# Loading the last two V of a two-block decode attention into the K tiles instead of the V ring

## The chip, the cores and the metric

One core of one Trainium2 chip. The metric is the device time of one launch in microseconds (us). The kernel before takes 1975.22 us (median of 3 runs: 1973.39 to 1975.72).

## The reference

Two independent decode attentions, A and B, with the same shapes; the results are concatenated. One query per batch row, so K and V, 805 MB of bf16 in all, are read once and used once.

```python
# per block: B=2, Sq=1, D=640, H=32 heads, Sk=8192, Dh=192
q = (x @ wq).reshape(B, 1, H, Dh)
scores = einsum("bhqd,bhkd->bhqk", q, k_cache) * Dh ** -0.5
p = softmax(scores)
o = einsum("bhqk,bhkd->bhqd", p, v_cache).reshape(B, 1, H * Dh) @ wo
```

## The kernel before

A *unit* is one head of one batch row of one block: 2 x 32 x 2 = 128 units, 0 to 127. "K126" is the K of unit 126, 3.1 MB laid out as 128 partitions x 64 keys x 192. Per unit, VectorE and ScalarE form the scores from K (VectorE multiplies, products `d1a` and `d1b`, then sums), the softmax follows, and TensorE (PE) makes 32 matmuls of the weights with V. All K and V go through SyncE's DMA queue, into two K tiles and two V tiles used in turn.

```python
kb = [sb(f"kb{i}", [128, T, Dh], BF16) for i in range(NK)]   # NK = 2
vb = [sb(f"vb{i}", [128, T, Dh], BF16) for i in range(NV)]   # NV = 2
# ... cut ...
def pe_pv(u, j0, j1):                      # 32 matmuls of a unit, or a part of them
    b = u % B
    vv = vb[u % NV][:].rearrange("p (j a) d -> p j (a d)", a=2)
    def fn(eng):
        for j in range(j0, j1):
            ins = eng.matmul(ops[(u // B) % 2][0:33, b, 0:QW], pb[u % NPB][:, j, :], vv[:, j, :],
                             start=(j == 0), stop=(j == T // 2 - 1))
        return ins
# ... cut: a V tile may be filled again when the matmuls that read it are done ...
def add_v(u):
    pc = pieces(u)
    w = [key("pv", u - NV)]
    if pc is None:
        S_sp.add(sp_v(u), waits=w)
    else:
        for (t0, t1, sm) in pc:            # the last four units: in 2, 2, 4 and 5 parts,
            S_sp.add(sp_v(u, t0, t1, sm), waits=w)    # each with a semaphore of its own
# ... cut: order on SyncE: K of unit u, then V of unit u-3; at the end
#     K127, V124, V125, V126, V127. K of unit u waits for d1b of unit u-2.
```

Of the kernel before, what the change touches and what calls it, by code (L numbers as in the profile page):

```python
# [102 lines left out]
def build_kernel(nc, blocks, out, cfg=None):  # L103
# [10 lines left out]
    NU = G * B  # L114
# [6 lines left out]
    NK = cfg.get("NK", 2)  # L121
    NV = cfg.get("NV", 2)
# [8 lines left out]
    def unit(u):  # L131
        g = u // B
        return g // Hn, g % Hn, u % B, g
# [14 lines left out]
    with ExitStack() as es:  # L148
# [4 lines left out]
        kb = [sb(f"kb{i}", [128, T, Dh], BF16) for i in range(NK)]  # L153
        vb = [sb(f"vb{i}", [128, T, Dh], BF16) for i in range(NV)]
# [34 lines left out]
        vsem = [sem(f"vsem{i}") for i in range(NV)]  # L189
# [9 lines left out]
        def key(name, *idx):  # L199
            for i in idx:  # L200
                if i < 0:
                    return None
            return (name,) + tuple(idx)
# [13 lines left out]
        def pieces(u):  # L217
            if u not in PCS:
                return None
            n0, cuts = PCS[u]  # L220
            ends = [c * T // 64 for c in cuts]
            return [(t0, t1, vtail[n0 + i]) for i, (t0, t1) in enumerate(zip([0] + ends[:-1], ends))]
# [15 lines left out]
        def dma(out_ap, in_ap, s):  # L238
            return lambda eng: eng.dma_start(out_ap, in_ap).then_inc(s, 16)  # L239
# [25 lines left out]
        def sp_k(u, part=None):  # L265
# [6 lines left out]
                return dma(kb[u % NK][:, 0:ks, :], src[:, 0:ks, :], ksem[u % NK])  # L272
            return dma(kb[u % NK][:, ks:T, :], src[:, ks:T, :], KSPLIT[u])

        def sp_v(u, t0=0, t1=None, sm=None):
            blk, h, b, g = unit(u)
            src = blocks[blk]["v"][b, h].rearrange("(p t) d -> p t d", p=128)
            if t1 is None:
                return dma(vb[u % NV][:], src, vsem[u % NV])
            return dma(vb[u % NV][:, t0:t1, :], src[:, t0:t1, :], sm)  # L280

        def xbc_copy(blk, b):
            return lambda eng: eng.tensor_copy(xbc[blk][b][:], xT[blk][b][:].unsqueeze(2).broadcast_to([128, DC, 128]))
# [87 lines left out]
        def pe_p0(qg):  # L371
            pr, b = qg // 2, qg % 2
            g0 = 2 * pr
            blk = g0 // Hn
            w = g0 // HG
            npr = HG // 2

            def at(slot, off):
                def fn(eng):
                    for c in range(DC):  # L380
                        ins = eng.matmul(qps[:, 0:QW], xbc[blk][b][:, c, :],  # L381
                                         wqs[:, slot, c, off].rearrange("p a n -> p (a n)") if slot is not w % 2 else
                                         wqs[:, slot, c, off],
                                         start=(c == 0), stop=(c == DC - 1))
                    return ins
                return fn
            fn = at(w % 2, slice((pr % npr) * QW, (pr % npr + 1) * QW))
            fn.same = (blk, b)
            fn.turn = lambda it: at(bass.ds((it + pr) // npr % 2, 1), bass.ds((it + pr) % npr * QW, QW))
            return fn, [("wq", w) if w == 0 else None, ("wq0b",) if (w == 0 and WQSPLIT and pr % npr >= 1) else None,  # L390
                        ("xbc", blk), key("a0", qg - 1)]

        def pe_pv(u, j0, j1):
            b = u % B
            vv = vb[u % NV][:].rearrange("p (j a) d -> p j (a d)", a=2)

            def fn(eng):
                for j in range(j0, j1):
# [3 lines that stand above are left out]
            fn.same = (j0, j1)  # L402
            return fn
# [52 lines left out]
        for u in range(NU):  # L456
            g = u // B
            put(dve_tab, u + 1, 0, dve_d3(u), [("acc", u), ("r", u), key("ar", u - 2)], ("d3", u))
            put(dve_tab, u, 2, dve_d1a(u), [("k", u), ("a0", qg_of(u)), key("acc", u - 2)], ("d1a", u))
            put(dve_tab, u, 3, dve_d1b(u), [("k", u), ("kb", u) if u in KSPLIT else None, ("a0", qg_of(u)),  # L460
                                            key("r", u - 1)], ("d1b", u))
            put(dve_tab, u, 4, dve_lvl(u, 96), [("d1b", u)], ("l1", u))
            put(dve_tab, u, 5, dve_lvl(u, 48), [("l1", u)], ("l2", u))
            put(dve_tab, u, 6, dve_lvl(u, 24), [("l2", u)], ("l3", u))
            put(dve_tab, u, 7, dve_r(u), [("l3", u), key("d3", u - 2), key("exp", u - 2)], ("r", u))
            put(pool_tab, u + 1, 0, pool_ar(u), [("d3", u), key("nb", u - 2)], ("ar", u))
            put(pool_tab, u + 1, 1, pool_ls(u), [("exp", u), key("f2", g - 2)], ("ls", u))
            put(act_tab, u + 1, 0, act_nb(u), [("ar", u), key("exp", u - 2)], ("nb", u))
            put(act_tab, u + 1, 1, act_exp(u), [("nb", u), ("acc", u), ("r", u), key("pv", u - NPB)], ("exp", u))
            for t in range(na_of(u)):  # L470
                w = [("d1a", u), key("d3", u - 2), key("exp", u - 2)] if t == 0 else []
                put(act_tab, u, 10 + t, act_acc(u, t), w, ("acc", u) if t == na_of(u) - 1 else None)
            pc = pieces(u)
            w0 = [("exp", u), key("f1", g - 2), ("init",)]
            if pc is None:
                put(pe_tab, u + LATE, 0, pe_pv(u, 0, T // 2), w0 + [("v", u)], ("pv", u))
            else:
                for i, (t0, t1, sm) in enumerate(pc):
                    put(pe_tab, u + LATE, 0, pe_pv(u, t0 // 2, t1 // 2), (w0 if i == 0 else []) + [("vp", u, i)],
                        ("pv", u) if i == len(pc) - 1 else None)  # L480
# [15 lines left out]
        for pp in range(G // 2):  # L496
# [13 lines left out]
            w = [("f4", pp), key("f5", pp - 1)]  # L510
# [8 lines left out]
        for qg in range(NQG):  # L519
            fn, w = pe_p0(qg)  # L520
# [4 lines left out]

        def add_v(u):
            pc = pieces(u)
            w = [key("pv", u - NV)]
            if pc is None:
                S_sp.add(sp_v(u), waits=w)  # L530
            else:
                for (t0, t1, sm) in pc:
                    S_sp.add(sp_v(u, t0, t1, sm), waits=w)
# [15 lines left out]
        for kind, u in korder:  # L549
            if kind == "k":  # L550
                if u in KSPLIT:
                    S_sp.add(sp_k(u, 0), waits=[key("d1b", u - NK)])
                    S_sp.add(sp_k(u, 1))
                else:
                    S_sp.add(sp_k(u), waits=[key("d1b", u - NK)])
                if u == 0:
                    if WQSPLIT:
                        S_sp.add(sp_wq(0, 1))
                    for blk in range(1, NBLK):
                        for b in range(B):  # L560
                            S_sp.add(sp_x(blk, b))
                w = u // UG
                if u % UG == (5 if UG >= 8 else 1):
                    S_sp.add(sp_wo(w), waits=[key("f5", (w - 1) * HG // 2)])
                if u % UG == (3 if UG >= 8 else 0) and w + 1 < NWG:
                    S_sp.add(sp_wq(w + 1), waits=[key("pq", w * HG)])
            else:
                add_v(u)
# [43 lines left out]
def bass_concat_heads__gqa_block_cached__mha_block_cached__decode_kernel(  # L612
    nc: bass.Bass,
    A_x: bass.AP,
    A_k_cache: bass.AP,
    A_v_cache: bass.AP,
    A_wq: bass.AP,
    A_wo: bass.AP,
    B_x: bass.AP,
    B_k_cache: bass.AP,  # L620
    B_v_cache: bass.AP,
    B_wq: bass.AP,
    B_wo: bass.AP,
    out: bass.AP,
):
    blocks = [
        dict(x=A_x, k=A_k_cache, v=A_v_cache, wq=A_wq, wo=A_wo),
        dict(x=B_x, k=B_k_cache, v=B_v_cache, wq=B_wq, wo=B_wo),
    ]
    build_kernel(nc, blocks, out)  # L630
# [28 lines left out]
```

## Time and profile before

| what | number | from |
|---|---|---|
| median time | 1975.22 us | timed runs |
| bytes over the span | 837 MB at 424 GB/s | page |
| V125 issued, its last part landed | 1933.34; 1948.38 us | timeline, chain |
| V126 and V127 issued | 1943.88; 1951.23 us | instruction records of SyncE |
| PE from the landing of V125 to the end of unit 127 | 1948.43 to 1966.58 us | chain |
| end | 1973.2 us | page |

Three lines of the page of the kernel before: the span, the rate in 40 slices of 49 us, and the shares of the chain that ended last (the profile goes back from the last instruction, at each step to what released it).

```profile
span 1973.2 us, 18371 instructions
...
GB/s 384 425 428 427 431 426 429 431 427 430 426 430 430 426 430 427 431 431 424 431 428 429 429 426 432 427 428 426 432 430 426 428 427 432 430 426 429 431 430 292
...
DMA 72%; PE 22%; DVE 5%; issue 1%; SPq 0%; ACT 0%; DVEq 0%
```

Transfers run at about 430 GB/s from the second slice to the last but one. Next, the last 25 us of the chain (start us, length us, what):

```profile
1933.71 14.67 DMA vb<-in_B_v_cache_dram
...
1948.43 2.78 PE ops L399 x16
1951.20 2.18 PE oTps L408 x12
1953.38 6.99 PE ops L399 x32
1960.37 0.91 PE outps L435 x6
1961.27 5.31 PE ops L399 x32
1966.58 1.36 PE oTps L419 x18
...
1970.87 0.43 ACT out_sb L363
```

The DMA piece is V125's second half. From 1948.43 on, no DMA: second half of unit 125, the transposes of an earlier pair of heads (L408), unit 126, that pair's output product (L435), unit 127, then the rest. Finally, busy time by stretches of 4 us (stretch, length, PE, weight load, VectorE, ScalarE, GpSimd, granted PE clock, DMA share, GB/s), and what SyncE's queue did (start, stretch covered by its issues) and waited for from 1930 us on:

```profile
1938.00:1942.00 4.00, 4.00 (x18) 2.01 (x17) 3.97 (x2) 2.45 (x15) 0.00 (x0) 0.69 1.00 423
1942.00:1946.00 4.00, 3.01 (x20) 1.63 (x18) 3.86 (x6) 0.00 (x0) 0.00 (x0) 1.00 0.57 181
1946.00:1950.00 4.00, 3.17 (x20) 1.74 (x19) 0.29 (x2) 0.64 (x3) 0.73 (x2) 1.00 0.99 394
...
1954.00:1958.00 4.00, 4.00 (x16) 1.99 (x15) 0.00 (x0) 0.67 (x2) 0.00 (x0) 0.57 0.98 375
1958.00:1962.00 4.00, 4.00 (x26) 2.13 (x25) 0.00 (x0) 0.64 (x2) 0.00 (x0) 1.00 0.90 359
```

```profile
1943.88 9.73 SPq L239 DMA_DIRECT2D vb<-in_B_v_cache_dram  x9
```

```profile
SPq L239 <- PE ops L399: 28.3, 3, 13.3
```

There is a hole: DMA is 0.57 busy and moves 181 GB/s (bytes counted where packets start; spread over the packets it is 193) in 1942 to 1946, because V126 may not go out before unit 124's matmuls have left its tile. That is what the change goes for.

### The profile page before, as it was taken

What the parts mean: (1) busy time and instruction counts of PE and PEld (TensorE: products, weight loads), DVE (VectorE), ACT (ScalarE), POOL (GpSimd) and SP (SyncE); (2) the same over time, 40 slices, a digit from 0 to 9 for tenths busy, and PEclk for the clock granted to TensorE, in tenths of its full rate; (3) what the DMA queues carried; (4) which work ended last, traced back from release to release, by engine and by line L of the source; (5) the groups of instructions that cost most, each with busy time, mean ns of one, the idle gap of its engine ahead of it and who ended that gap; (6) DMA issues with size and microseconds to landing.
All of it is one profiled execution on the core that took longest, in us unless ns stands there. A gap on an engine that the chain in (4) does not pass through costs nothing.

```text
span 1973.2 us, 18371 instructions
## 1 busy us (share of the span) xinstructions
PE 1116.4 (57%) x5004; PEld 591.5 (30%) x5004; DVE 1655.5 (84%) x962; ACT 904.1 (46%) x4743; POOL 152.7 (8%) x270
## 2 busy tenths in 40 slices
PE   2546546655655555655655656556555565555657
PEld 1223223322333323322332323223232332223324
DVE  7889898888878888888888888888788887888884
ACT  4445454445445444454444444444445444544442
POOL 4013030000000000000000000000000000000000
PEclk9777777777777777777777777777777776777778
DMA  9999999999999999999999999999999999999997
GB/s 384 425 428 427 431 426 429 431 427 430 426 430 430 426 430 427 431 431 424 431 428 429 429 426 432 427 428 426 432 430 426 428 427 432 430 426 429 431 430 292
DMA packets 56477, 837.12 MB, mean 424 GB/s; under 512 B 7417, under 2 KB 18305, under 8 KB 23681
## 3 DMA queue, kind: packets, MB, share of 16 engines
q1 hardware_dynamic: 56432, 836.79, 99.7%
q8 instruction: 12, 0.20, 0.0%
q14 instruction: 17, 0.13, 0.0%
q10 hardware_dynamic: 16, 0.01, 0.0%
HBM read 836.77 MB, written 0.01 MB: 424 GB/s over the span
## 4 chain that ended last, share of the span: by engine, by line
DMA 72%; PE 22%; DVE 5%; issue 1%; SPq 0%; ACT 0%; DVEq 0%
DMA vb<-in_B_v_cache_dram 36%; DMA vb<-in_A_v_cache_dram 29%; PE ops L399 22%; DMA kb<-in_A_k_cache_dram 7%; DVE prodD L303 3%; DVE prodD L310 1%; DVE prodA L299 0%; DVE sc L314 0%; PE oTps L408 0%; PE oTps L419 0%; PE outps L435 0%; SPq L239 0%; SPq L246 0%; DVE mp L306 0%; ACT oTzL L353 0%
## 5 line engine op out<-in xcount | busy, mean ns | idle before, releaser
L399 PE MATMUL ops<-vb,pb 128*33 128x384 bf16 x4096 | 953.2, 408 | 786.7 <-DMA vb<-in_B_v_cache_dram 395.8
L399 PEld LDWEIGHTS ops<-vb,pb 128*33 128x33 bf16 x4096 | 481.4, 120 | 1248.8 <-DMA vb<-in_B_v_cache_dram 414.0
L321 ACT ACTIVATE prodA<-prodA 128x192 bf16<-128x192 bf16 x2048 | 709.1, 350 | 119.0 <-DVE prodA L299 118.6
L303 DVE TENSOR_TENSOR prodD<-kb,qbc 128x9216 bf16<-128x9216 bf16 x128 | 633.7, 4951 | 3.5 <-DMA kb<-in_A_k_cache_dram 3.5
L310 DVE TENSOR_TENSOR prodD<-prodD 128x4608 bf16<-128x4608 bf16 (+2 forms) x384 | 598.9, 1560 | 13.3
L299 DVE TENSOR_TENSOR prodA<-kb,qbc 128x3072 bf16<-128x3072 bf16 x128 | 224.9, 1757 | 250.5 <-DMA kb<-in_B_k_cache_dram 133.4
L321 ACT ACTIVATION_READ_ACCUMULATOR prodA<-prodA 128x1 f32 x2048 | 386.8, 189 | 0.0
L325 ACT ACTIVATE nb<-mg 128x1 f32<-128x1 f32 x128 | 26.0, 203 | 742.2 <-POOL mg L286 742.2
L286 POOL PARTITION_ALL_REDUCE mg<-mp x128 | 57.7, 451 | 1668.7 <-DVE mp L306 1668.7
L314 DVE TENSOR_REDUCE sc<-prodD 128x48 f32<-128x1152 bf16 x128 | 173.1, 1353 | 4.4
L290 POOL PARTITION_ALL_REDUCE lall<-rs x128 | 84.2, 658 | 114.7 <-ACT pb L328 114.7
L335 ACT ACTIVATE o_sb<-ops 1x384 f32<-1x384 f32 x63 | 30.1, 477 | 87.4 <-PE oTps L408 73.3
L408 PEld LDWEIGHTS oTps<-ones,o_sb 33*128 33x128 f32 x372 | 67.1, 257 | 9.8 <-issue 9.8
L408 PE MATMUL oTps<-ones,o_sb 33*128 33x1 f32 x372 | 69.7, 311 | 0.0
L359 ACT ACTIVATE qbc<-qps 128x384 bf16<-128x384 f32 x64 | 31.3, 489 | 79.0 <-PE qps L381 78.3
L328 ACT ACTIVATE pb<-sc,nb 128x64 bf16<-128x64 f32 x128 | 52.2, 408 | 16.6 <-ACT nb L325 8.3
L381 PE MATMUL qps<-wqs,xbc_1 128*128 (+1 forms) x160 | 34.8, 352 | 40.7 <-ACT qbc L359 40.7
L381 PE MATMUL qps<-wqs,xbc_0 128*128 (+1 forms) x160 | 33.2, 340 | 11.8 <-DMA wqs<-in_A_wq_dram 11.8
L306 DVE TENSOR_REDUCE mp<-sc 128x1 f32<-128x64 f32 x128 | 28.1, 220 | 13.9 <-issue 5.0
L435 PE MATMUL outps<-wos,oTz 128*4 (+1 forms) x186 | 31.1, 304 | 14.0 <-ACT oTz L353 14.0
L381 PEld LDWEIGHTS qps<-wqs,xbc_1 128*128 128x128 bf16 x160 | 13.8, 102 | 58.9 <-ACT qbc L359 42.9
L336 ACT ACTIVATE o_sb<-ops 1x384 f32<-1x384 f32 x63 | 30.4, 482 | 0.7
(29 smaller groups left out, 96.2 us busy)
## 6 DMA issues: line engine op xcount, KB each, us to landing
vb<-in_A_v_cache_dram SPq DMA_DIRECT2D x64, 3072.0 KB, 22.4
kb<-in_B_k_cache_dram SPq DMA_DIRECT2D x64, 3072.0 KB, 23.2
kb<-in_A_k_cache_dram SPq DMA_DIRECT2D x63, 3072.0 KB, 22.6
vb<-in_B_v_cache_dram SPq DMA_DIRECT2D x60, 3072.0 KB, 23.0
wos<-in_A_wo_dram SPq DMA_DIRECT2D x8, 960.0 KB, 27.1
wqs<-in_B_wq_dram SPq DMA_DIRECT2D x8, 960.0 KB, 24.8
wos<-in_B_wo_dram SPq DMA_DIRECT2D x8, 960.0 KB, 27.2
wqs<-in_A_wq_dram SPq DMA_DIRECT2D x7, 960.0 KB, 24.8
```

Of the source, the lines that this page charges most:

```text
L286: return lambda eng: eng.partition_all_reduce(mg[u % 2][:], mp[u % 2][:], 128, bass.bass_isa.ReduceOp.max)
L290: return lambda eng: eng.partition_all_reduce(lall[g % 2][:, b:b + 1], rs[u % 2][:], 128, bass.bass_isa.ReduceOp.add)
L299: return lambda eng: eng.tensor_tensor(prodA[u % 2][:, 0:na, :], kb[u % NK][:, 0:na, :], qb_bc(u, na), ALU.mult)
L303: return lambda eng: eng.tensor_tensor(prodD[:, 0:T - na, :], kb[u % NK][:, na:T, :], qb_bc(u, T - na), ALU.mult)
L310: return lambda eng: eng.tensor_tensor(prodD[:, 0:nd, 0:w], prodD[:, 0:nd, 0:w], prodD[:, 0:nd, w:2 * w], ALU.add)
L314: return lambda eng: eng.tensor_reduce(sc[u % 2][:, na:T], prodD[:, 0:T - na, 0:24], AXL.X, ALU.add)
L321: return lambda eng: eng.activation(prodA[u % 2][:, t, :], prodA[u % 2][:, t, :], ACTF.Identity, accum_out=sc[u % 2][:, t:t + 1])
L328: return lambda eng: eng.activation(pb[u % NPB][:, :, ::32], sc[u % 2][:].rearrange("p (j a) -> p j a", a=2), ACTF.Exp, bias=nb[u % 2][:], ...
L359: return lambda eng: eng.activation(qbc[qg % 4][:], qps[:, 0:QW].rearrange("p (a d) -> p a d", a=2), ACTF.Identity)
L381: ins = eng.matmul(qps[:, 0:QW], xbc[blk][b][:, c, :], wqs[:, slot, c, off].rearrange("p a n -> p (a n)") if slot is not w % 2 else wqs[:, ...
L399: ins = eng.matmul(ops[(u // B) % 2][0:33, b, 0:QW], pb[u % NPB][:, j, :], vv[:, j, :], start=(j == 0), stop=(j == T // 2 - 1))
L408: ins = eng.matmul(oTps[:, 2 * i + b:2 * i + b + 1], o_sb[:, b, :, :].rearrange("p s (r i) -> p i (s r)", i=3)[:, i, :], ones33[:], start= ...
```

## The change

When V126 and V127 are due, both K tiles are free for good: the last K have been multiplied. So these two V go there, and wait for `d1b` of their own unit instead of for the matmuls two units back. Nothing is added: the same transfers, bytes and instructions.

```diff
+        def v_tile(u):
+            return kb[u % NK] if NU >= 8 and u >= NU - 2 else vb[u % NV]
+
         def sp_v(u, t0=0, t1=None, sm=None):
...
-            return dma(vb[u % NV][:, t0:t1, :], src[:, t0:t1, :], sm)
+            return dma(v_tile(u)[:, t0:t1, :], src[:, t0:t1, :], sm)
...
-            vv = vb[u % NV][:].rearrange("p (j a) d -> p j (a d)", a=2)
+            vv = v_tile(u)[:].rearrange("p (j a) d -> p j (a d)", a=2)
...
-            w = [key("pv", u - NV)]
+            w = [("d1b", u)] if NU >= 8 and u >= NU - 2 else [key("pv", u - NV)]
```

More of the change, by code (lines that the diff above doesn't have):

```diff
@@ L278, in sp_v @@
             if t1 is None:
-                return dma(vb[u % NV][:], src, vsem[u % NV])
-            return dma(vb[u % NV][:, t0:t1, :], src[:, t0:t1, :], sm)
+                return dma(v_tile(u)[:], src, vsem[u % NV])
+            return dma(v_tile(u)[:, t0:t1, :], src[:, t0:t1, :], sm)
         def xbc_copy(blk, b):
```

## The prediction

> **What bounds the kernel now.** The transfers: the page shows 424 GB/s over the span, the DMA row at 9 in all slices but the last, and a chain that is 72% DMA and 22% PE. From 1870 to 1934 us the packets run at 422 to 431 GB/s[...]. The change touches only the last 40 us.
>
> **The tail, from timeline, landings and packets.** SyncE issues V125 at 1933.34 (after the matmuls of unit 123), V126 at 1943.88 (after unit 124's), V127 at 1951.23 (after unit 125's). The packets show a hole: 193 GB/s in 1942 to 1946 instead of about 430, so about 2.2 us of transfer time. That is what the change aims at.
>
> **What it moves.** V126 then waits for the product of K126 (ended 1925.1), V127 for that of K127 (ended 1939.6). SyncE is in order, so V126 still comes behind V125: about 1934.2 (V125's two issues take 0.8 us), 9.7 us earlier; V127 at 1939.7, 11.5 us earlier. No instruction, byte or SBUF is added.
>
> **How much of that is critical: by my reading nothing.**
> 1. V125's second half landed on fifteen engines at 1942.8 to 1945.5, on one at 1948.4. That one never ran dry: its landings go on at 3.67 us per 1.5 MB and 1.85 to 1.9 us per 0.75 MB straight through the hole, no faster while the fifteen stood still. V126's parts count as landed only with it. So the last landings of V126 and V127 (1950.2 to 1955.9; 1957.7 to 1963.6) hardly move; the fifteen only arrive earlier.
> 2. Even an earlier landing has no taker. From 1948.43 PE never waits for data: 2.78 us second half of unit 125, 2.18 us L408, 6.99 us unit 126 (first part landed 3.1 us before), 0.91 us L435, 5.31 us unit 127 to 1966.58, about 2.2 us behind its data, then an end of about 5 us. The chain of waits holds no DMA after 1948.38. That landing, V125's, the last that counts, is not touched: its issue still waits for unit 123, and what is queued behind it drains after it.
>
> **Predicted.** 1974.9 us, within 1972.5 to 1977.0; measured runs before spread from 1973.39 to 1975.72. Chances: faster by over 2% 0.004, within 2% 0.992, slower by over 2% 0.004 (2% is 39 us, the whole tail).
>
> **What would show it.** Right: V126 issued near 1934.2, V127 near 1939.7; no slice under 370 GB/s between 1934 and 1958; last landings of V126's and V127's parts within 0.7 us of before while the first come 2 to 3 us earlier, so the spread in the last transfers grows from 2.3 us to 4 or more; the chain after V125's landing the same PE groups, with no DMA. Wrong: the last parts landing 2 us earlier (the engines share one limit; point 1 falls, point 2 still keeps the time), or the end of unit 127's matmuls moving by more than the PE clock's steps explain.
>
> **What could make it wrong.** The granted PE clock steps between 0.5 and 1.0 in this tail (unit 126 took 6.99 us, unit 127 5.31), so another phase moves the end by 1 to 3 us either way. More queued behind V125 could slow its slow engine and push 1948.38 later, one for one. If the slow engine owes its lag to chance, runs differ by a few us whatever the change.

That SyncE issues in order is what the run of the change shows: K126's product ended at 1925.30, but V126 went out at 1934.31, right behind V125's two issues (1933.46 to 1934.26).

## The result

1975.22 us median (1973.56 to 1975.45, 4 runs) against 1974.7 us (1973.39 to 1975.72, 4 runs) before: ratio 1.0001, 95% interval 0.9984 to 1.0018. A ratio is the mean time of one kernel's runs over that of the other's runs of the same rounds, so it is not quite the ratio of the medians. The class is "same", as predicted.

The change did just what it was built to do. The same views of the changed kernel (its line numbers are three higher: L402 is L399 of before). The page:

```profile
span 1973.5 us, 18371 instructions
...
GB/s 384 425 429 427 430 426 431 430 425 430 428 430 430 426 431 427 430 430 426 430 426 430 429 427 431 428 427 428 430 431 428 429 428 430 430 426 430 431 429 290
...
DMA 72%; PE 22%; DVE 5%; issue 1%; SPq 0%; ACT 0%; DVEq 0%
```

The stretches, SyncE's issues, and its waits:

```profile
1938.00:1942.00 4.00, 4.00 (x18) 1.95 (x17) 3.97 (x2) 2.67 (x16) 0.00 (x0) 0.69 1.01 423
1942.00:1946.00 4.00, 2.98 (x19) 1.64 (x18) 3.90 (x5) 0.00 (x0) 0.00 (x0) 1.00 0.99 407
1946.00:1950.00 4.00, 3.14 (x20) 1.68 (x18) 0.47 (x4) 0.64 (x3) 0.73 (x2) 1.00 1.01 414
...
1954.00:1958.00 4.00, 4.00 (x16) 1.99 (x15) 0.00 (x0) 0.95 (x3) 0.00 (x0) 0.57 0.98 398
1958.00:1962.00 4.00, 4.00 (x27) 2.12 (x25) 0.00 (x0) 0.64 (x2) 0.00 (x0) 1.00 0.21 84
```

```profile
1934.31 11.44 SPq L239 DMA_DIRECT2D kb<-in_B_v_cache_dram  x9
```

```profile
SPq L239 <- PE ops L402: 13.3, 1, 13.3
SPq L239 <- DVE prodD L306: 3.4, 1, 3.4
```

V126 is issued at 1934.31 instead of 1943.88, V127 at 1939.89 instead of 1951.23, and the hole is filled: 407 GB/s instead of 181. The bytes moved forward come off the end, where 359 GB/s becomes 84. And the chain:

```profile
1933.83 14.82 DMA vb<-in_B_v_cache_dram
...
1948.70 2.78 PE ops L402 x16
1951.48 2.18 PE oTps L411 x12
1953.66 6.99 PE ops L402 x32
1960.65 0.91 PE outps L438 x6
1961.55 5.31 PE ops L402 x32
1966.86 1.35 PE oTps L422 x18
...
1971.15 0.43 ACT out_sb L366
```

It is the same chain to a hundredth of a microsecond from V125's landing on. No DMA follows V125's landing in either chain, and PE's pieces are end to end.

The landings say why the data did not come earlier either. Every K and V transfer of the two kernels has 16 landing records, which I read as one for each of the 16 DMA engines that the page counts. The kernel waits for all 16: PE starts on V125's second half at 1948.43, 0.05 us after the 16th landing and 2.97 us after the 15th. From those records (us):

| transfer | before: first, 15th, 16th | after: first, 15th, 16th |
|---|---|---|
| V125, second half | 1942.8, 1945.5, 1948.4 | 1942.9, 1945.4, 1948.7 |
| V126, first part | 1947.8, 1948.4, 1950.2 | 1944.8, 1947.2, 1950.5 |
| V126, last part | 1953.4, 1955.3, 1955.9 | 1950.5, 1952.9, 1956.2 |
| V127, last part | 1961.4, 1963.2, 1963.6 | 1958.1, 1960.4, 1963.6 |

Fifteen engines are 1 to 3 us earlier. The sixteenth is where it was: it was behind the others by enough to have had work right through the hole. (The records don't name the engine. That it is one and the same is inferred from the last landings, which in the kernel before go on through the hole at an even pace: 3.67 and 3.68 us for the halves of V125, 1.85, 1.90, 1.88 and 1.85 us for the quarters of V126.)

### The profile page after: what moved, and what is told of

Read it like the earlier page. It is cut to its first block, busy times and chain, and to the rows that moved or that the text cites. A ratio compares the mean times of both kernels' runs of the same rounds, so it can differ in the third digit from the quotient of the medians.

```text
span 1973.5 us, 18371 instructions
## 1 busy us (share of the span) xinstructions
PE 1111.1 (56%) x5004; PEld 589.3 (30%) x5004; DVE 1655.7 (84%) x962; ACT 904.1 (46%) x4743; POOL 151.5 (8%) x270
## 4 chain that ended last, share of the span: by engine, by line
DMA 72%; PE 22%; DVE 5%; issue 1%; SPq 0%; ACT 0%; DVEq 0%
DMA vb<-in_B_v_cache_dram 36%; DMA vb<-in_A_v_cache_dram 29%; PE ops L402 22%; DMA kb<-in_A_k_cache_dram 7%; DVE prodD L306 3%; DVE prodD L313 1%; DVE prodA L302 0%; DVE sc L317 0%; PE oTps L411 0%; PE oTps L422 0%; PE outps L438 0%; SPq L239 0%; SPq L246 0%; DVE mp L309 0%; ACT oTzL L356 0%
## 5 line engine op out<-in xcount | busy, mean ns | idle before, releaser
L402 PE MATMUL ops<-vb,pb 128*33 128x384 bf16 x4032 | 935.4, 407 | 792.5 <-DMA vb<-in_B_v_cache_dram 398.5
L402 PEld LDWEIGHTS ops<-vb,pb 128*33 128x33 bf16 x4032 | 472.6, 120 | 1246.1 <-DMA vb<-in_B_v_cache_dram 416.6
L384 PE MATMUL qps<-wqs,xbc 128*128 (+1 forms) x320 | 67.9, 346 | 51.7 <-ACT qbc L362 40.0
L384 PEld LDWEIGHTS qps<-wqs,xbc 128*128 128x128 bf16 x320 | 27.1, 101 | 87.0 <-ACT qbc L362 42.2
L331 ACT ACTIVATION_READ_ACCUMULATOR pb<-sc,nb 128x1 f32 x128 | 23.8, 186 | 0.0
## 6 DMA issues: line engine op xcount, KB each, us to landing
wqs<-in_B_wq_dram SPq DMA_DIRECT2D x8, 960.0 KB, 24.8
wqs<-in_A_wq_dram SPq DMA_DIRECT2D x7, 960.0 KB, 24.8
```

What stands on the lines that cost most here:

```text
L331: return lambda eng: eng.activation(pb[u % NPB][:, :, ::32], sc[u % 2][:].rearrange("p (j a) -> p j a", a=2), ACTF.Exp, bias=nb[u % 2][:], ...
L384: ins = eng.matmul(qps[:, 0:QW], xbc[blk][b][:, c, :], wqs[:, slot, c, off].rearrange("p a n -> p (a n)") if slot is not w % 2 else wqs[:, ...
```

## The experiments

The kernels have hardware loops that wait on semaphores against register values, and the experiments were confined to waits against constants. So every experiment has its loops written out (`emit(eng)` instead of `emit(eng, 8)` or `emit(eng, 4)`), and the written-out kernels before and after are the base. That base differs in one way that turned out to matter, below. "To the end" always means from the last landing of V125 to the end of the span, in the profiled run; it shakes off what happens earlier. Results and ratios against the looped kernel before of the same rounds:

| run | median us (range) | ratio | V125 to V127, last landings, us | V125 to the end, us |
|---|---|---|---|---|
| before, looped | 1974.70 (1973.39 to 1975.72) | | 15.25 | 24.8 |
| after, looped | 1975.22 (1973.56 to 1975.45) | 1.0001 | 14.95 | 24.8 |
| u_before | 1994.95 (1992.96 to 1996.02) | 1.0098 | 15.42 | 24.8 |
| u_after | 1994.33 (1993.60 to 1995.21) | 1.0100 | 15.03 | 23.1 |
| c_before | 1994.51 (1994.04 to 1994.80) | 1.0102 | 15.58 | 24.2 |
| c_after | 1994.62 (1994.51 to 1995.07) | 1.0104 | 14.98 | 23.6 |
| n_after | 1993.36 (1992.70 to 1994.55) | 1.0098 | none | 23.1 |
| n124_after | 1989.74 (1989.13 to 1989.98) | 1.0079 | 16.00 | 24.0 |
| r_before | 1994.53 (1993.92 to 1995.03) | 1.0100 | 15.73 | 24.1 |
| r_after | 1993.91 (1993.25 to 1994.96) | 1.0100 | 15.04 | 23.1 |
| nr_after | 1990.45 (1989.71 to 1991.04) | 1.0079 | none | 20.3 |
| d_before | 2023.20 (2019.65 to 2026.04) | 1.0251 | 15.83 | 23.5 |

The intervals of the ratios are about 0.0017 either way. Two more kernels, i_before and p_before, had one run each, of unknown state.

**Theory A.** After V125's last landing PE is serial to the end, so V126 and V127 have no taker that waits; and one DMA engine lags, so they would not land earlier anyway. **Rivals.** The data are the limit and something offset a gain; or the data did come earlier and only busy PE hid it; or the lag of that engine is chance.

### u_before and u_after: loops written out

```diff
-                S_dve.emit(eng, 8)
+                S_dve.emit(eng)
```
(the same for ScalarE and PE)

> The kernel before with its three hardware loops written out (the loops wait on register values, which no new run may do); it is to be the base of the other runs, and a test of why one DMA engine lags. Theory A (the lag is made by instruction fetches, which in both traces add about 0.67 us to one engine each time an 8 KB fetch packet appears): about 1.2 MB of instructions are fetched instead of 0.33 MB, some 100 packets more, so the last of the 16 landings trails the others far more or the stream as a whole slows, and the time rises by 20 to 90 us. Theory B (that engine is slow by chance or by place, fetches have nothing to do with it): 1975 within 5 us, last landing about 3 us behind the others as before.

> The changed kernel with its loops written out. Both theories of the result (PE is serial after V125's last landing; or the lagging engine sets the last landing of V127): equal to the written-out kernel before within 0.3%, V126 and V127 issued about 10 us earlier than there. A rival (the change gains, but the kernel as given happens to hide it) would show it faster by 2 us or more.

Measured: 1994.95 and 1994.33 us. The change is worth nothing here either (the ratios differ by 0.0002). That u_after's stretch to the end is 1.7 us shorter in the profiled run is PE's clock: unit 126 took 6.99 us in u_before with a granted clock of 0.76 in that stretch, and 5.31 us in u_after at 1.00. The clock records have only 0.5 and 1.0, in stretches that are multiples of 3.4 us (249 of 250 in before and in after; the last one is cut by the end of the trace), and one such stretch of 3.4 us at 0.5 accounts for the 1.7 us: it makes a mean of 0.76 over 6.99 us.

Writing the loops out cost 19.5 us, just under the 20 to 90 us of theory A (1.06 MB of instructions were fetched in 61 packets more than the looped kernel's, where the estimates were 1.2 MB and 100) and far outside theory B's 5 us. This run alone does not show that the fetches are the cause; see d_before.

### c_before and c_after: PE's work at the end cut

```diff
-                for j in range(j0, j1):
+                for j in ((j0, j1 - 1) if u >= NU - 2 else range(j0, j1)):
```

> Kernel before, written out, with the matmuls of units 126 and 127 cut to the first and the last of each part: 18 instead of 64, some 9 us of PE work less at the end (wrong result on purpose). Is PE the limit of the tail? Theory A (PE serial after V125's last landing, 24.8 us from there to the end in the base): PE now catches up and the end follows V127's last landing by about 7 us, so 22 to 22.5 us after V125's landing, about 2.5 us less than the base, and not 9 less. Rival (the last transfer sets the end already): no change.

> The changed kernel, written out, with the same cut. Now the data decide the end in both. Theory A (the engine that lags never ran dry, so the earlier issue moves its landings by nothing): V127's last landing 15 us after V125's and the end 22 to 22.5 us after it, the same as the cut kernel before within 0.7 us. Rival (the change does bring the data 2 us earlier, and only busy PE hid it): about 2 us shorter than the cut kernel before.

Their outputs are wrong, which doesn't matter for the times. With 46 of 64 matmuls gone, both chains have V127's landing in them (10.93 us and 20.84 us of DMA before the last matmuls; c_before, then c_after), so now data decide:

```profile
1973.14 10.93 DMA vb<-in_B_v_cache_dram
```

```profile
1963.25 20.84 DMA kb<-in_B_v_cache_dram
```

The changed kernel is 0.6 us quicker from V125's to V127's last landing (14.98 against 15.58), not 2 us: within the 0.7 us of theory A. The times are the same. The expected 22 to 22.5 us to the end were missed (24.2 and 23.6): PE's clock was lower, 0.50 throughout 1975 to 1990 us in c_before with PE busy for 10.50 of the 15 us, against 0.89 and 14.11 us in u_before, and the last product (L435) took 1.77 us instead of 0.99. Part of what the cut took from PE was lost again at the lower clock.

### n_after and n124_after: transfers taken away behind V125, and ahead of it

```diff
         def add_v(u):
             pc = pieces(u)
+            if u >= NU - 2:          # n124_after: u == NU - 4
+                return
```
(and the matmuls of these units don't wait for the parts; wrong result)

> The changed kernel, written out, without the transfers of V126 and V127 at all; the matmuls read the K that lies in those tiles (wrong result on purpose). 6.3 MB less, which is 14.6 us at 430 GB/s. Theory A: the end stays 23 to 25 us after V125's last landing, the time stays within 2 us of the written-out changed kernel. Rival (transfers bound the tail): faster by 5 us or more.

> The changed kernel, written out, without the transfer of V124 (its matmuls read what is in the tile; wrong result on purpose): 3.1 MB less, but ahead of V125. A positive control. Theory A (V125's last landing is what counts): V125 lands 5 to 7 us earlier and the time falls by 5 to 7 us, from half the bytes whose removal behind V125 gave nothing. Rival (bytes don't matter in the tail, PE alone does from earlier on): under 2 us.

Measured: without V126 and V127, 6.3 MB less, 1993.36 us, 1.0 us under u_after, ratio 1.0098 against 1.0100; 23.1 us to the end, as with them. Without V124, half as many bytes, 1989.74 us, 4.6 us less, with V125's last landing at 1963.33 instead of 1968.72 us. So 3.1 MB ahead of V125 cost 4.6 us, and 6.3 MB behind it 1.0 us, which lies inside the ranges. The gain was 4.6 us rather than the 5 to 7 expected, because with V125 5.4 us earlier V127's third part became the limit. Its landing is the last DMA in the chain of n124_after:

```profile
1960.88 16.56 DMA kb<-in_B_v_cache_dram
```

This run also shows a tail without the lag: with V124 gone all engines caught up before V125, whose 15th and 16th landings came together (1963.31 and 1963.33 us). V127 still landed 16.00 us after V125 (a lag of 0.9 us arose within it), so the data behind V125 took no less time without a straggler at the start than with one (15.0). There is no such run of the kernel before, so what the change is worth without the lag is not shown. The chain of n_after from V125 on:

```profile
1954.82 13.51 DMA vb<-in_B_v_cache_dram
...
1968.37 2.78 PE ops L402 x16
1971.14 2.18 PE oTps L411 x12
1973.33 5.31 PE ops L402 x32
1978.63 0.91 PE outps L438 x6
1979.54 5.31 PE ops L402 x32
```

It is the chain of the kernel with the transfers: PE cannot tell that they are missing.

### r_before and r_after: 3.1 us of PE moved to where it waits anyway

L408 and L435 of the last but one pair of heads sit between units 125, 126 and 127, though their inputs are ready long before. Here they run before units 124 and 125. The result is right.

```diff
-                put(pe_tab, at, 1, pe_f3, ...
+                e = pp == LASTP - 1
+                put(pe_tab, at - e, -1 if e else 1, pe_f3, ...
-                put(act_tab, at + 2, 3, act_f4(pp), ...
+                put(act_tab, at if e else at + 2, 50 if e else 3, act_f4(pp), ...
-            put(pe_tab, at + 1, 2, pe_f5(pp), w, ("f5", pp))
+            put(pe_tab, at if e else at + 1, -1 if e else 2, pe_f5(pp), w, ("f5", pp))
```

> Kernel before, written out, with the L408 and L435 groups of the last but one pair (2.18 and 0.91 us of PE) moved ahead of unit 124's and unit 125's matmuls, where PE waits for data anyway. Correct result. Theory A (PE is serial after V125's last landing): from there to the end 22 to 23 us instead of 23.1 to 24.8, the rest taken by the wait for V127's last landing; so 1 to 2 us faster than the written-out kernel before (1.0098 of the looped one), to about 1.009. Rival (something else than PE and V127 sets the end): no change in that stretch.

> The changed kernel, written out, with the same move: if the change has any worth, here it shows, since PE is 3 us quicker. Theory A: the engine that lags still sets V127's landing, so at most 0.7 us shorter than the run above, within noise. Rival (the change brings data 2 us earlier and PE hid it): 2 us shorter than the run above.

Measured: 1994.53 and 1993.91 us, ratios 1.0100 both; the expected 1.009 was missed, and so were the 22 to 23 us to the end (r_before took 24.1). The 0.6 us between them lie inside the ranges. V125's to V127's landing took 15.73 and 15.04 us: again 0.7 us for the change. r_after needs 23.1 us to the end, as u_after. That it is the same number is in part chance: unit 127's matmuls end 0.6 us sooner after V125's landing, and the last product takes 1.57 instead of 0.99 us. The rest of what it saved on PE it waits for:

```profile
1961.33 20.29 DMA kb<-in_B_v_cache_dram
...
1981.66 2.78 PE ops L402 x16
1984.43 1.35 PE oTps L422 x18
```

Now the landing of V127's third part is in the chain. So two limits of about the same length lie side by side after V125: PE's work, and the landings of V126 and V127 with what follows. (The stretch to the end is the same 23.1 us in u_after, n_after and r_after.)

### nr_after: both at once

> The changed kernel, written out, with both at once: no transfer of V126 and V127 (wrong result on purpose), and L408 and L435 of the last but one pair moved ahead. Each alone left 23.1 us from V125's last landing to the end. Theory A (two limits of nearly the same length lie side by side there: PE's work, and V127's landing plus its rest): together they take the 3.1 us of L408 and L435 out, so 20.0 to 20.5 us, and the time falls by about 3 us against the written-out changed kernel. Rival (a third limit, not PE and not the data): still about 23 us.

The edits of n_after and r_after together (wrong result). 20.3 us to the end, and 1990.45 us, 3.9 us under u_after:

```profile
1957.42 8.28 PE ops L402 x32
1965.69 0.91 PE outps L438 x6
1966.60 15.71 PE ops L402 x96
1982.31 1.35 PE oTps L422 x18
```

PE is now serial already from V124's first landing. Taking either limit away gave nothing clear of noise, taking both gave 3 to 4 us (1990.45 against 1993.36, 1993.91 and 1994.33). That bounds what a change of the last two V could have been worth in this tail with PE's work in either of these two orders: about 0.2% of the time.

### d_before: why one engine lags

In the traces of before and after, the last landing's distance from the eighth of its transfer (its lag) stays constant for hundreds of microseconds and then steps up. (It also fell, from 4.1 to 2.9 us between 430 and 1120 us in before.) In before, late in the run: 2.89 us at 1841.5, 3.54 at 1849.5, 4.23 at 1894.0, 4.98 at 1941.0. Instruction packets of 8 KB on DMA queue 14 start at 1844.7, 1892.0 and 1939.0, just ahead of these steps. (One more, at 1918.0, has no step; of ten such packets after 150 us five have one, so "each time" in the expectation of u_before was too strong.) In u_before, from 300 to 1945 us: of 38 intervals between the last landings of one K or V and the next with one such packet, 26 have a step of 0.5 to 0.9 us (median 0.65); of 172 without one, none has. The test is to add fetches and nothing else: instructions that move no data, on an engine with time to spare (ScalarE was busy for 904.8 us, 45%, of u_before).

```diff
+            if 8 <= u < 120:
+                put(act_tab, u, 40, act_nops, [], None)   # 40 x eng.sem_inc(dummy, 1)
```

> Kernel before, written out, plus 40 increments of an unused semaphore on ScalarE after the score rows of units 8 to 119: 4480 instructions that move no data, about 35 more 8 KB fetch packets if one takes 64 bytes. ScalarE has 5 us or more to spare per unit. Theory A (each 8 KB fetch holds one DMA engine up by about 0.65 us, and the slowest engine paces the stream): 15 to 25 us slower than the written-out kernel before, so a ratio of 1.017 to 1.023. Theory B (fetches don't matter): 1.010 as without them.

Measured: 2023.2 us, 28.3 us over u_before (29.3 when each is set against the looped kernel of its own rounds), ratio 1.0251. The instruction queues' lines (packets, MB, share), of the pages of before, u_before and d_before in turn:

```profile
q8 instruction: 12, 0.20, 0.0%
q14 instruction: 17, 0.13, 0.0%
```

```profile
q8 instruction: 39, 0.64, 0.1%
q14 instruction: 51, 0.42, 0.1%
```

```profile
q8 instruction: 39, 0.64, 0.1%
q14 instruction: 86, 0.70, 0.1%
```

Queue 14 rises by 34 packets and the time by 19.5 us (0.57 us each, with queue 8 rising too), then by 35 packets, as predicted, and the time by 28.3 us (0.81 us each). (35 packets of 8 KB for 4480 instructions are 64 bytes each, the size that the expectation took; queue 8's packets, 12 with 0.20 MB in before, are of 16 KB.) The direction and the count are as theory A said; the size is above its 15 to 25 us. A lag step is 0.65 us, which would make 23 us of 35 packets. The two profiled executions, the only ones with packets on record, do differ by 23.6 us (2019.65 and 1996.02), 0.68 us a packet; why the other three of d_before took 2.5 to 6.4 us more is not shown. Theory B is out: it had no increase at all. The rival that the increments cost ScalarE's time finds no support in the traces: the other engines' waits for ScalarE sum to 219 us in u_before and in d_before.

The engine's own pace shows it more plainly than the lag. From 300 to 1950 us the last landings of successive K and V are 7.31 us apart (9.7 where weights come between). With one fetch packet in the interval, 30 of 38 in u_before and 60 of 68 in d_before are longer by 0.5 to 1.0 us (median 0.68); without one, none of 173 and 140 is longer by over 0.4. Eight stay unmoved in each kernel, so not every fetch meets this engine, but the added ones nearly all do. The lag in u_before grows from 4.1 us at 296 to 12.2 us at 1084 and then stays between 10.7 and 12.9, though the fetches go on, and the rate of the page's slices, 425 to 432 GB/s from the second to the 19th, is 415 to 430 from the 20th to the 39th (from 947 us on). From about there, as I read it, the others wait for the slow engine, and that is where the time goes; no run shows that wait itself. In the looped kernels it never passes 5.1 us.

How a fetch holds the engine up is not shown by any run here.

### i_before and p_before: one inconclusive, one a partial answer

> The kernel before with the loops over units written out, but the 28 middle matmuls and the 12 middle score rows of a unit put into small loops without waits: fewer instructions fetched than written out in full (PE about 2.5 times fewer), more register work per matmul. Theory A: time between the kernel before and the fully written-out one. Theory B: the time differs from the written-out one only if PE becomes the limit (its matmuls would then take over 12 us per unit instead of 7.5).

The small loops (two matmuls per turn, `bass.ds` addresses):

```diff
+                    with eng.bass.Fori(0, T // 2 // RG - 2, ...) as it:
+                        for k in range(RG):
+                            jj = bass.ds(it * RG + (RG + k), 1)
+                            eng.matmul(..., pb[u % NPB][:, jj, :]..., vv[:, jj, :]..., start=False, stop=False)
```

Measured: 2141.15 us, one run. PE was busy 1668 us (13.0 us per unit, over the 12 estimated as the mark where PE may be the limit), and the fetches did not fall but rose, to 124 packets on queue 8 and 259 on queue 14. Nothing can be concluded on either theory.

> A probe, correct result: the kernel before, written out, with ten of the 128 V (units 40 to 96) loaded in two or three transfers of fewer partitions (120 and 8, 104 and 24, 126 and 2 and so on)[...]. Theory A (one fixed DMA engine serves the instruction fetches and lags for it): the parts that don't use that engine land without a straggler, those that do have one landing 2 us or more behind their others[...]. Theory B (whichever engine is last changes from transfer to transfer): stragglers in all parts or in no orderly subset. Time 1995 to 2040, since uneven parts hold up the stream.

That some of these parts would spare the lagging engine was the assumption.

```diff
+        VPART = {40: [(0,120),(120,128)], 46: [(0,104),(104,128)], 52: [(0,126),(126,128)], ...}
```

Measured: 2248.45 us, one run, far outside the expected 1995 to 2040; why uneven parts hold the stream up that much is not settled. The landings answer the question asked in part: each of the 23 parts, down to those of two and three partitions, has one landing 13 to 28 us behind the next to last. The parts of two partitions have 3 landing records instead of 16, the first of them 0.4 us after the issue; which engines a part went over, the records don't say, so which one the straggler is was not shown. No split by partitions tried here was without a straggler, so a whole kernel without the lag could not be tried.

### A version that beats both

None was found. r_after is right and the best of the written-out correct kernels, but writing the loops out costs 19.5 us, and it does not differ from u_after by more than the noise. The same reordering on the looped kernel was not run.

## Why the prediction was right

- **Time.** 1974.9 predicted, 1975.22 measured; the class "same" had 0.992. The time tests little: 2% is 39 us, the whole tail, and even if the whole hole of 2.2 us had been won, the median would have been 1972.5 (1974.7 less 2.2), at the edge of the range given. The landings and the chain are what test the mechanism.
- **What it moves.** V126 near 1934.2 and V127 near 1939.7 predicted; 1934.31 and 1939.89 measured. The hole is gone: the lowest 4 us stretch from 1934 to 1958 has 398 GB/s. (In slices of 1 us, two are just under the 370 named: 369 at 1934, as before the change, and 366 at 1957.)
- **Point 1, the engine that never ran dry.** The last landings of V126's and V127's parts are all within 0.3 us of before, while the first come 2.9 to 3.3 us earlier, and the spread of the last transfer grew from 2.3 to 5.6 us. Measured from V125's landing, the four pairs (looped, u, c, r) give the change 0.3, 0.4, 0.6 and 0.7 us: a small real gain in the data, out of a hole of 2.2 us.
- **Point 2, no taker.** Shown by n_after: removing these transfers altogether, not only advancing them, leaves the stretch to the end at 23.1 us. The prediction put PE some 2.2 us behind its data; r_after showed what that means, that 3.1 us less PE work runs into V127's landing and gains nothing clear of noise. So "PE is the limit" was right but near an edge.
- **A term that was off.** "An end of about 5 us" after unit 127's matmuls is 6.6 us in both kernels (1966.58 to 1973.2). It was mis-sized by 1.6 us and had no effect, since the change does not touch it.
- **A worry that did not hold.** That the lag might be chance: most of its steps come with instruction fetches (in u_before, from 300 to 1945 us, all 26), and adding fetches added time (d_before). The other two, PE's clock and a slower V125 from more queued behind it: the clock did move the end by 1.7 us between u_before and u_after, in the range given; V125's landing came 0.28 us later in the profiled run and its issue 0.12 us later, so any slowing is under 0.2 us in this pair.

## What to carry to other kernels

The hole in the DMA rate was worth here only what the last engine to land lost in it, 0.3 to 0.7 us of 2.2: look at all 16 landings, not at the mean rate, before paying for earlier issues. Then ask who waits for the data that would come earlier; the test that settled it here was to remove the transfer altogether (wrong result, one kernel). In this stream of 420 GB/s over the span (u_before), 35 added fetch packets, nearly all of which met the engine that lands last (by its last landings, 60 of 68 intervals in d_before, 30 of 38 in u_before), delayed the whole kernel by 24 to 28 us.
